# Moving the third h of a slot behind the next slot's W1 in a fused convolution and mixer kernel on Trainium2

## The chip, the cores and the metric

The kernel runs on one core of one Trainium2 chip. The metric is the device time of one execution in microseconds (us). Before the change the median of four runs is 327.03 us (326.15 to 327.87).

## What is computed

Two stages are fused. A causal convolution runs over the sequence with 7 taps per head (softmax of `weight`, 8 heads of 24 channels). Its output goes through a mixer with a low-rank part along the sequence and a two-layer part along the channels. Shapes: 8 batches, 4224 positions, 192 channels; rank 32, hidden width 768.

```python
w = softmax(weight, axis=-1)                      # 8 heads, 7 taps
y[b, s, h, :] = sum_k w[h, k] * x_pad[b, s + k, h, :]   # 6 zero rows ahead of x
xt = y.transpose(0, 2, 1)
h = xt @ U @ V                                    # rank 32, along the sequence
u = y + h.transpose(0, 2, 1)
out = u + np.maximum(u @ w_ch1, 0.0) @ w_ch2
```

## The kernel before, in words

**Tiles and groups.** The 8 x 4224 positions are cut into 264 tiles of 128 positions, 33 to a batch. Eight tiles make a group, so there are 33 groups (0 to 32), and some span two batches. For each batch there is a convolution (`c`), the product with U summed over the whole sequence (`t` and `s`), and for each group there are three steps:

- **h** (`h_group`, line 484, which calls `h_tiles`, line 442): eight matmuls (L453), two tiles to a PSUM bank, so four banks, or five where the first tile of the group is odd in its batch or the group spans two batches. Then VectorE adds y to each bank and writes u in bf16 (L475): one add for two tiles, or single adds where a run of four tiles ends. `transp` (L494) then issues one transposing DMA on SyncE's queue (SP), which gives uT.
- **W1** (`w1`, line 538): 36 matmuls of 512 columns (L550) from uT, in 12 banks, each cleared by a relu on ScalarE (L564) or VectorE (L566) after the pattern `RELU` (7 banks on ScalarE and 5 on VectorE).
- **W2** (`w2`, line 573): a group is done in four pieces. Each has 12 matmuls (L579) into one bank, one VectorE add of u that writes the output tile (L588), and one output DMA on SP (L596).

**Buffers.** All PSUM tiles come from one pool of 8 banks (`bank`, line 56), taken in turn in the order of the calls. A matmul into a bank waits until the tile that held it eight calls earlier has been read. u has 7 buffers, uT 5, y 3, relu outputs 3, output tiles 8.

**The order of the work is written out by hand** (`manual_schedule`). The list `SLOTS` (line 615) has 14 entries, counted here from 0. An entry names the groups whose W1 is run, then the groups whose W2 is run, and a dictionary of what stands ahead of which W2 piece. From slot 5 on a slot has W1 of three groups (3k-9 to 3k-7 for slot k), then the twelve W2 pieces of the same groups. The loop at line 786 runs W1 first, then for each position p what the dictionary gives for p, then piece p. In the codes `h9` is the h of group 9, `c4:0:3:AAD` the convolution of batch 4 for three heads from head 0 with its banks read by ScalarE, ScalarE, VectorE in turn (`conv32`, line 317: two banks and eight matmuls, L335, for each head; the reads are L252 and L254), `t4` and `s4` the low-rank sum, `x5:3` the first shifted copies of x on GpSimd. In slots 6 to 9 the convolution stands at positions 1, 2 and 3 (three, three and two heads), in slots 4 and 5 at 2, 3 and 4.

Before the change slot k, from 5 to 9, makes the h of groups 3k-5, 3k-4 and 3k-3 at positions 5, 8 and 11; position 11 is ahead of the last piece. Slot 4 makes h9 at position 11. Slots 10 to 12 have h at positions 0, 4 and 8.

**Loads.** x of a later batch is loaded by GpSimd's queue in four parts (`x_load`, L79), each held until a given block of W1 has ended (`LOADS`, line 666). Behind each load one more step of the shifted copies runs on GpSimd (L289, L301).

Of the kernel before, what the change touches and what calls it, by code (L numbers as in the profile page):

```python
# [14 lines left out]
def kernel(  # L15
# [590 lines left out]
    def x_load(b, q, after):  # L606
        if q == 0:
# [20 lines left out]
                6: ["t2"],  # L628
                8: ["s2"],
                9: ["h8"],  # L630
                11: ["h9"],
            },
        ),
    ]
    nh = 10
    for k in range(5, 14):
        gs = list(range(3 * k - 9, 3 * k - 6))
        hs = [f"h{g}" for g in range(nh, min(nh + 3, NG))] + [None] * 3
        nh = min(nh + 3, NG)
        if k == 5:  # L640
            at = {
                2: ["c3:0:3:AAD"],
                3: ["c3:3:3:AAD"],
                4: ["c3:6:2:A", "x4:3"],
                5: [hs[0]],
                6: ["t3"],
                8: ["s3", hs[1]],
                11: [hs[2]],
            }
        elif k < 10:  # L650
            b = k - 2
            at = {
                1: [f"c{b}:0:3:AAD"],
                2: [f"c{b}:3:3:AAD"],
                3: [f"c{b}:6:2:A"] + ([f"x{b + 1}:3"] if b + 1 < B else []),
                5: [f"t{b}", hs[0]],
                7: [f"s{b}"],
                8: [hs[1]],
                11: [hs[2]],
            }  # L660
        else:
            at = {0: [hs[0]], 4: [hs[1]], 8: [hs[2]]}
        SLOTS.append((gs, gs, {p: [w for w in what if w] for p, what in at.items()}))
# [176 lines left out]
```

## Time and profile before

| | |
|---|---|
| median of four runs | 327.03 us (326.15 to 327.87) |
| the profiled execution | 327.87 us, of which the profile's span is 326.1 us |
| granted TensorE clock, mean | 0.997 |
| TensorE weight loads | 223.6 us busy |
| ScalarE relu (L564) | 233 of 604 ns mean |
| VectorE relu (L566) | 163 of 688 ns mean |
| VectorE u add (L475) | 168 of 461 ns mean |
| VectorE output add (L588) | 133 of 551 ns mean |
| output DMAs | 131 issues, 2.9 us to landing |
| uT transposes | 31 issues, 4.1 us to landing |

The span runs from the first to the last instruction; the time of the run is a little longer than it. Busy time of an engine is what its instructions took. The chain that ended last follows the work back from the last instruction, at each step to what released it or to the instruction ahead of it on its engine. In the profile PE is the TensorE's matmuls, PEld its weight loads, DVE VectorE, ACT ScalarE, POOL GpSimd, SP SyncE; L550 is line 550.

### The profile page before, as it was taken

Reading aid. Unit: us, or ns where it says so; the run is one execution under the profiler, and the core shown is the slowest. Engines: PE = TensorE matmul, PEld = TensorE weight load, DVE = VectorE, ACT = ScalarE, POOL = GpSimd, SP = SyncE. Lnnn points to the kernel's source line nnn. Section 1 sums busy time; section 2 is a strip of 40 time slices with the busy share of each in tenths; the row PEclk is TensorE's granted clock in tenths of the full one; section 3 lists DMA queues with packets and bytes.
Section 4 is the critical chain, followed back from the end, with each engine's and each line's share of the span. In section 5 each row is a group of like instructions: output and inputs, shape, how many; then the busy total and the mean of one; then the engine's idle time right before and its main releaser. Section 6 shows DMA issues by size and latency. Waiting matters only on the chain.

```text
span 326.1 us, 9590 instructions
## 1 busy us (share of the span) xinstructions
PE 319.3 (98%) x3998; PEld 223.6 (69%) x3998; DVE 269.5 (83%) x552; ACT 170.0 (52%) x343; POOL 143.8 (44%) x112
## 2 busy tenths in 40 slices
PE   8999999999999999999999999999999999999994
PEld 3666676578677647866864784587796496497494
DVE  7659999986987987998798699879888888896853
ACT  1667524761775297088339609824904903903900
POOL 8584169717975894786859497000000000000000
PEclk9999999999999999999999999999999999999998
DMA  9999994999999999599799957139168079058044
GB/s 105 189 181 157 213 219 112 175 203 222 221 112 221 248 170 162 172 164 197 166 240 162 205 154 191 47 110 240 47 186 250 3 163 274 2 143 245 2 147 146
DMA packets 122907, 53.52 MB, mean 164 GB/s; under 512 B 87760, under 2 KB 122832, under 8 KB 122864
## 3 DMA queue, kind: packets, MB, share of 16 engines
q1 hardware_dynamic: 84528, 38.08, 48.0%
q0 software_dynamic: 38192, 14.73, 39.7%
q8 instruction: 31, 0.51, 0.6%
q14 instruction: 12, 0.10, 0.1%
q10 hardware_dynamic: 144, 0.10, 0.1%
HBM read 29.49 MB, written 25.95 MB: 170 GB/s over the span
## 4 chain that ended last, share of the span: by engine, by line
PE 91%; DVE 3%; DMA 3%; ACT 1%; issue 0%; POOL 0%; POOLq 0%
PE ps L579 41%; PE ps L550 39%; PE ps L335 3%; PE ps L453 3%; DMA x_sb<-in_x_dram 3%; PE ps L398 2%; DVE rl_sb L566 1%; ACT rl_sb L564 1%; DVE y_sb L254 1%; PE ps L365 1%; PE ps L505 1%; DVE u_sb L475 1%; PE ps L520 0%; ACT y_sb L252 0%; PE ps L678 0%
## 5 line engine op out<-in xcount | busy, mean ns | idle before, releaser
L564 ACT ACTIVATE rl_sb<-ps 128x512 bf16<-128x512 f32 x233 | 124.3, 604 | 108.0 <-PE ps L550 96.0
L579 PE MATMUL ps<-W_sb,rl_sb 128*128 128x192 bf16 x1584 | 141.9, 246 | 0.1
L579 PEld LDWEIGHTS <-rl_sb 128*128 128x128 bf16 x1584 | 128.0, 98 | 13.5 <-issue 13.0
L550 PE MATMUL ps<-uT,W_sb 64*128 64x512 bf16 x1188 | 131.8, 376 | 0.0
L566 DVE TENSOR_SCALAR rl_sb<-ps 128x512 bf16<-128x512 f32 x163 | 105.3, 688 | 15.7 <-PE ps L550 15.4
L550 PEld LDWEIGHTS <-W_sb 64*128 64x128 bf16 x1188 | 66.1, 94 | 61.4 <-issue 3.4
L588 DVE TENSOR_TENSOR out_sb<-ps,u_sb 128x384 f32<-128x384 f32 (+1 forms) x133 | 70.4, 551 | 25.8 <-PE ps L579 25.5
L301 POOL COPY xb_sb<-x_sb 32x3072 bf16<-32x3072 bf16 (+1 forms) x24 | 67.6, 2826 | 0.7
L475 DVE TENSOR_TENSOR u_sb<-y_sb,ps 128x192 bf16<-128x192 bf16 (+1 forms) x168 | 66.3, 461 | 0.0
L289 POOL COPY xb_sb<-x_sb 128x3072 bf16<-128x3072 bf16 x12 | 32.8, 2744 | 35.5 <-DMA x_sb<-in_x_dram 18.4
L252 ACT ACTIVATE y_sb<-ps 128x408 bf16<-128x408 f32 (+4 forms) x89 | 37.8, 512 | 11.1 <-PE ps L335 7.9
L79 POOL DMA_DIRECT2D x_sb<-in_x_dram x32 | 27.1, 851 | 16.9 <-PE ps L550 9.7
L254 DVE CAST y_sb<-ps 128x408 bf16<-128x408 f32 (+4 forms) x37 | 19.6, 578 | 1.4 <-PE ps L365 1.3
L453 PE MATMUL ps<-tt_sb,V_sb 32*128 32x192 bf16 x264 | 12.4, 246 | 0.2 <-DVE y_sb L254 0.2
L335 PE MATMUL ps<-xb_sb,band 64*32 64x384 bf16 x192 | 12.1, 332 | 0.0
L335 PE MATMUL ps<-x_sb,band 64*32 64x384 bf16 x192 | 12.1, 333 | 0.0
L453 PEld LDWEIGHTS <-V_sb 32*128 32x128 bf16 x264 | 4.7, 92 | 7.5 <-issue 7.5
L155 PE MATMUL ps<-zz 128*128 128x512 f32 x12 | 8.3, 846 | 1.5 <-DVE zz L145 1.5
L412 ACT ACTIVATE tt_hi<-ps 128x192 bf16<-128x192 f32 x8 | 2.6, 331 | 11.2 <-PE ps L398 11.1
L365 PE MATMUL ps<-x_sb,band 64*64 64x240 bf16 (+3 forms) x192 | 8.0, 275 | 0.4 <-DMA x_sb<-in_x_dram 0.4
L365 PEld LDWEIGHTS <-band 64*64 64x64 bf16 x192 | 6.0, 106 | 2.2 <-issue 1.8
L335 PEld LDWEIGHTS <-band 64*32 64x32 bf16 x384 | 4.5, 89 | 4.1 <-issue 3.0
(65 smaller groups left out, 73.8 us busy)
## 6 DMA issues: line engine op xcount, KB each, us to landing
out_dram<-out_sb SPq DMA_DIRECT2D x131, 192.0 KB, 2.9
x_sb<-in_x_dram POOLq DMA_DIRECT2D x14, 384.0 KB, 7.8
x_sb<-in_x_dram POOLq DMA_DIRECT2D x7, 432.0 KB, 7.8
x_sb<-in_x_dram POOLq DMA_DIRECT2D x7, 408.0 KB, 9.3
x_sb<-in_x_dram POOLq DMA_DIRECT2D x1, 504.0 KB, 8.8
uT<-u_sb SPq DMA_TRANSPOSE x31, 4.1
x_sb<-in_x_dram POOLq DMA_DIRECT2D x1, 480.0 KB, 5.8
W_sb<-in_moe_w_ch_dram POOLq DMA_DIRECT2D x2, 192.0 KB, 7.0
```

The costliest lines, as they stand in the source:

```text
L79: return nc.gpsimd.dma_start(out=xt[b][HB * r : HB * r + HB, s0:s1, :], in_=x[b, blk * HB : (blk + s1 - s0) * HB, :].rearrange("(j p) d -> ...
L252: nc.scalar.activation(out=out, in_=in_, func=ACT.Copy)
L289: nc.gpsimd.tensor_copy(out=xbt[b][:, s0:s1, :], in_=xt[b][:, s0 + 1 : s1 + 1, :])
L301: nc.gpsimd.tensor_copy(out=xbt[b][q, s0:s1, :], in_=xt[b][q, s0:s1, :])
L335: nc.tensor.matmul(out=pp[r][QB * cg : QB * cg + QB, 0 : nk[r] * GS], lhsT=w[hr], rhs=t[hr, st : st + 2 * nk[r] - 1 : 2, hs], start=True, ...
L453: nc.tensor.matmul(out=banks[pr][:, a * D : (a + 1) * D], lhsT=V_sb[32 * q : 32 * q + 32, (j // 8) * 2 + j % 2, :], rhs=ttb[b][32 * q : 32 ...
L475: nc.vector.tensor_tensor(out=u_group(g)[:, i : i + n, :, hf, :], in0=yt[b][:, run[0] : run[0] + n, :].rearrange("p n (c k) -> p n c k", c=3),
L550: last = nc.tensor.matmul(out=pps[m][hf][:], lhsT=W1_sb[HB * hf : HB * hf + HB, c, m * P : (m + 1) * P], rhs=uTt[g][HB * hf : HB * hf + HB ...
L564: nc.scalar.activation(out=rl[:, m, hf, :], in_=pp[hf][:], func=ACT.Relu)
L566: nc.vector.tensor_scalar_max(out=rl[:, m, hf, :], in0=pp[hf][:], scalar1=0.0)
L579: last = nc.tensor.matmul(out=cps[:, a * D : (a + 1) * D], lhsT=rlt[g][:, m, hf, (i + a) * P : (i + a + 1) * P], rhs=W2_sb[:, m, :], start ...
L588: nc.vector.tensor_tensor(out=o[:, 0:n, :].rearrange("p n (c k) -> p n c k", c=3), in0=cps[:, 0 : n * D].rearrange("p (n c k) -> p n c k", ...
```

## The change

Two things are changed in the table that orders the work. In slots 5 to 9 the h that stood at position 11 is no longer there, and one stands at position 0, between the last W1 and the first W2 piece of the slot. `nh`, the number of the first h that slot 5 makes, is 9 instead of 10, and slot 4 no longer has h9. So each h that stood at position 11 of a slot (groups 9, 12, 15, 18, 21, 24) stands at position 0 of the next one. The groups at positions 5 and 8 stay what they were. In slots 10 to 12 the numbers of the h are one lower at each position, and slot 12 has h32 at position 8 in place of 4. No instruction is added or taken away.

```diff
                 8: ["s2"],
                 9: ["h8"],
-                11: ["h9"],
             },
         ),
     ]
-    nh = 10
+    nh = 9
     for k in range(5, 14):
...
                 4: ["c3:6:2:A", "x4:3"],
-                5: [hs[0]],
+                0: [hs[0]],
+                5: [hs[1]],
                 6: ["t3"],
-                8: ["s3", hs[1]],
-                11: [hs[2]],
+                8: ["s3", hs[2]],
             }
         elif k < 10:
             b = k - 2
             at = {
+                0: [hs[0]],
                 1: [f"c{b}:0:3:AAD"],
                 2: [f"c{b}:3:3:AAD"],
                 3: [f"c{b}:6:2:A"] + ([f"x{b + 1}:3"] if b + 1 < B else []),
-                5: [f"t{b}", hs[0]],
+                5: [f"t{b}", hs[1]],
                 7: [f"s{b}"],
-                8: [hs[1]],
-                11: [hs[2]],
+                8: [hs[2]],
             }
```

## The prediction

> **What bounds the kernel now.** I read the busy table, then the chain that ended last, then single stretches of the timeline. Slots are numbered by their place in the list `SLOTS`, from 0; a "piece" is one call of `w2` (12 matmuls, 192 columns each).
>
> The page gives busy time by engine and the chain's shares:
>
> ```profile
> PE 319.3 (98%) x3998; PEld 223.6 (69%) x3998; DVE 269.5 (83%) x552; ACT 170.0 (52%) x343; POOL 143.8 (44%) x112
> ...
> PE 91%; DVE 3%; DMA 3%; ACT 1%; issue 0%; POOL 0%; POOLq 0%
> ```
>
> TensorE (PE) is the chain. From 69.20 us to 321.69 us the chain has no entry but PE, save 0.01 us of issue. So a moved step can gain only what PE loses next to it, and loses whatever PE is made to wait. The chain in order of time (start, length, what) gives the slots; L550 is W1, L579 a piece, L335 a convolution, L453 an h:
>
> ```profile
> 110.93 11.76 PE ps L550 x108
> 122.69 1.10 PE ps L579 x12
> 123.78 0.64 PE ps L335 x19
> 124.42 1.10 PE ps L579 x12
> ...
> 137.60 0.28 PE ps L453 x8
> 137.88 1.10 PE ps L579 x12
> 138.97 11.92 PE ps L550 x108
> ...
> 223.50 11.84 PE ps L550 x108
> 235.34 0.28 PE ps L453 x8
> 235.62 4.07 PE ps L579 x48
> ...
> 260.13 0.44 PE ps L453 x8
> 260.57 4.07 PE ps L579 x48
> ```
>
> The reader is to see three things. An h at the end of a slot costs PE its own 0.28 us (0.35 where its group spans two batches: 109.48 and 222.05). The W1 behind it takes 11.76 to 11.92 us. In slots 10 to 12 an h already stands right behind W1, and four pieces follow it without loss.
>
> **What the change moves.** No work is added or removed: 33 h, the same matmuls, adds and transposes. In slots 4 to 9 the h of position 11 (h9, h12, h15, h18, h21, h24) goes to position 0 of the next slot, past the last piece and three W1. Positions 5 and 8 keep the same groups. In slots 10 to 12 the h at positions 0, 4, 8 have numbers one lower, and h32 gets position 8 of slot 12.
>
> **What goes: the burst on VectorE (DVE) ahead of W1.** Its adds (about 2 us) run into W1's first microseconds there. Six W1 stand behind such an h, in slots 5 to 10: 11.92, 11.76, 11.92, 11.76, 11.76, 11.84 us. The W1 of slots 11 to 13, without one, take 11.76 each. The gain is 0.16 + 0.16 + 0.08 = **0.40 us** for the kernel, and it is also the most that these rows allow.
>
> **What comes: a burst on DVE right behind W1, and PSUM banks that are held by it.** The 8 banks go round in the order of the calls. After W1 the h takes 4 banks (h9, h18) or 5 (h12, h15, h21, h24, whose first tile is odd or which span two batches). The first piece takes one, and the convolution of three heads takes six. So the piece behind the convolution is the twelfth or thirteenth to ask, and gets the bank of the h's last add; two of the convolution's heads get h banks too. DVE first ends W1's relus, then does the adds, then the first piece's output. When do the adds end? Four slots already have h behind W1:
>
> - slot 10, four adds: h starts at 235.27, adds end 235.98 + 1.94 = 237.92, so 2.65 us after h's start
> - slot 12, six adds: 285.02 to 285.76 + 2.07 = 287.83, 2.81 us
> - slot 11, five adds: 2.75 us; slot 4, six adds: 65.90 to 66.61 + 2.07, 2.78 us
>
> In slots 10 to 12 four pieces follow h at once and ask only for free banks; that is why nothing is lost there. Slot 4 has a convolution after two pieces, and there the trace shows the mechanism. This is its timeline (start, length, engine, line, operation):
>
> ```profile
> 65.90 0.35 PE L453 MATMUL ps<-tt_sb,V_sb 32*128 32x192 bf16 x8
> 66.18 2.15 PE L579 MATMUL ps<-W_sb,rl_sb 128*128 128x192 bf16 x24
> 66.61 2.07 DVE L475 TENSOR_TENSOR u_sb<-y_sb,ps 128x192 bf16<-128x192 bf16 x6
> ...
> 68.60 1.02 DVE L588 TENSOR_TENSOR out_sb<-ps,u_sb 128x384 f32<-128x384 f32 x2
> ...
> 68.74 0.35 PE L335 MATMUL ps<-x_sb,band 64*32 64x384 bf16 x2
> ...
> 69.20 1.15 PE L579 MATMUL ps<-W_sb,rl_sb 128*128 128x192 bf16 x12
> ```
>
> The adds end at 68.68 and the convolution's third head goes on at 68.74 (0.06 us later). The first output add ends near 69.11, and the piece that gets its bank starts at 69.20 (0.09 us later). The convolution begins at 68.26 and takes 0.64 us where nothing stops it, so the piece could have started at 68.90: 0.30 us are lost although two pieces (2.09 us) lie between.
>
> Now the slots of the change, in us after h's start. In **slots 6 to 9** only one piece stands ahead of the convolution. PE gets through h, piece and convolution in 0.28 + 1.10 + 0.64 = 2.02. The next piece can't start before the last add, 2.81 + 0.06 = 2.87 with six adds (slots 7, 9), so 0.85 is lost in each. Slot 6 has six adds too, but h12 cost 0.35 where it was, so 0.78. Slot 8 has four adds: 2.65 + 0.06 - 2.02 = 0.69. In **slot 5** two pieces lie ahead, as in slot 4, and the third needs the first one's output add: 2.65 + 0.51 + 0.09 = 3.25, against 0.28 + 2.09 + 0.64 = 3.01, so 0.24. A wait of 0.16 us for h's fifth bank (slot 11 has 0.44 for such an h, not 0.28) ends before the add does, and is inside these numbers. In slots 10 to 12 the exchange of numbers comes to nothing: slot 10 gets the five-bank h (+0.16), slot 11 loses it (-0.16).
>
> Is something late after that? With six adds DVE does output 0 until 3.3, two casts of the convolution (0.52 each) until 4.3, output 1 until 4.8. The third piece asks for a cast's bank at 2.87 + 1.10 + 0.64 = 4.6, and gets it by 0.3 us. I take nothing here; if that cover goes, a second stall like slot 4's (0.30) comes in four slots, 1.2 us.
>
> Sum: 0.24 + 0.78 + 0.85 + 0.69 + 0.85 = 3.41 lost, 0.40 gained: **+3.0 us**.
>
> **What else moves.** Each moved h issues a transpose on SP (SyncE's queue). There it stood ahead of the slot's last output; now it stands ahead of the new slot's first. SP holds it until the adds end (2.8), issues for 1.3 to 2.6 us (the 31 transposes of the trace), then sends output 0 at 4.1 to 5.4. Outputs land in 2.9 us and have 8 buffers, so the first reuse comes eight pieces later, past 10 us: hidden by some 2 us. The transposed group is wanted by W1 of the next slot, a slot (28 us) later than the h. On POOL the loads of x are tied to W1's ends, and the last shifted copy ends at 123.05 against the convolution's start at 123.71 in slot 6. The convolution moves 0.28 us away from it, so that margin grows. POOL's wait ahead of its next load (1.18 us in slot 6) shrinks by the 0.35 us of the removed h at most. ScalarE is idle 0.81 us ahead of the convolution. All these cost nothing; if the tightest, SP's, failed, outputs would hold up DVE by what is over 2 us.
>
> **Two rules weighed.** The row is the slot 4 loss of 0.30 us with all banks in rotation. The Trainium skill, page "Perfetto Trace Analysis", section "Optimizing Tensor Performance", says that matmul groups which rotate through banks have their evacuation overlapped by the next group's matmuls. By that alone the change would cost nothing and give -0.4; the row decides against it, as rotation helps only while DVE is less than eight banks behind. The same page, section "Identifying the Most-Contended Engine", holds matmul busy time to be a poor measure and takes weight-load busy instead, which is 69% here and would leave room to absorb a wait. The row is W1's 11.76 us in slots 6, 8, 9 and 11 to 13, the same with and without DVE's burst: PE is at its pace, so I take a wait on PE in full.
>
> **Rivals.**
> - **A, the wait for h's adds** (forecast): +3.0.
> - **B, it is mostly covered**, each of five slots losing no more than slot 4's 0.30: 1.5 - 0.4 = +1.1. For it: that loss is the only one measured with a convolution behind h. Against: slots 6 to 9 have 1.1 us less cover.
> - **C, not slower: the adds end in time.** Place: the second piece of slots 6 to 9. It decides if the last add ends within 2.0 us of h's start; then only W1's gain is left, -0.4. Against: 2.65 to 2.81 in four slots. If, beyond that, h filled PE's gap at W1's end (weights for the first piece wait 0.42 us there), six times 0.28 more, -2.1. Against: in slots 10 and 11 W1 keeps its length and h is paid in full behind it.
> - **D, the stall carries on** into the third piece (the 0.3 us cover gone): +4.2.
>
> **How the numbers follow.** The sum stands against the profiled execution: span 326.1, time 327.87, so 330.9 after, span 329.1. That execution is the slowest of four; against the median, 327.03, the forecast is 327.03 + 3.0 = **330.0 us**. By the same base B gives 328.1, C 326.6 (or 324.9), D 331.2. Chances: A 0.68, D 0.14, B 0.09, C 0.05, its larger form 0.04. The 0.5% that a measurement of this kernel can tell from no change is 1.6 us. A and D are slower (0.82), B and C within (0.14), the larger C faster (0.04). The range takes A, B and D: 328.0 to 331.5, with 0.3 us for the runs' spread above D.
>
> **What would show it.** In the changed profile: W1 of slots 5 to 10 at 11.76 us. Behind each W1 an h of 0.28 to 0.44, a piece, and then in slots 6 to 9 a gap on PE of 0.7 to 0.85 us in or behind the first convolution, ended by DVE's L475, which will appear on the chain some 3 us more. In slot 5 a gap of 0.2 to 0.3 us, ended by L588. The forecast is wrong if the second piece starts within 2.1 us of h's start, if the gap comes again behind the second convolution, or if W1 falls below 11.76.

## The result, and the profile after

The changed kernel takes 327.77 us (median of 53 runs, 326.97 to 329.20), the kernel before 326.73 us (median of 79). The ratio is 1.0027, 95% interval 1.0020 to 1.0034: slower by 0.9 us, where 3.0 were forecast (the medians differ by 1.0). The profiled execution took 327.67 us, span 325.9. A few executions were in a second, slower state; the ratios leave them out, the medians of the later table do not (two of six executions in after_sp_plus, one of twelve in before_shifted and in late_mix).

The page after, the lines that answer to those of before (busy time by engine; the chain's shares):

```profile
PE 319.8 (98%) x3998; PEld 216.1 (66%) x3998; DVE 270.6 (83%) x552; ACT 170.1 (52%) x343; POOL 143.7 (44%) x112
...
PE 91%; DVE 6%; ACT 1%; issue 1%
```

PE is as busy as before; DVE has doubled its share of the chain, a first hint that PE now waits for it. The chain of the changed kernel in order of time (start, length, what) shows slot 6 and the first part of slot 10:

```profile
109.48 11.76 PE ps L550 x108
121.25 0.47 PE ps L453 x8
121.71 1.10 PE ps L579 x12
122.81 0.37 PE ps L335 x5
123.18 0.49 ACT y_sb L252
123.66 0.04 issue
123.71 0.36 PE ps L335 x5
124.07 1.10 PE ps L579 x12
...
134.10 4.07 PE ps L579 x48
138.16 11.76 PE ps L550 x108
...
224.11 11.76 PE ps L550 x108
235.87 0.53 PE ps L453 x8
236.40 4.07 PE ps L579 x48
```

The convolution behind the first piece, 0.64 us before, now takes 1.26 (122.81 to 124.07). What holds it is seen in the timeline of the same stretch (start, length, engine, line, operation):

```profile
121.65 1.16 PE L579 MATMUL ps<-W_sb,rl_sb 128*128 128x192 bf16 x12
121.92 2.07 DVE L475 TENSOR_TENSOR u_sb<-y_sb,ps 128x384 bf16<-128x384 bf16 x6
...
123.16 1.68 ACT L252 ACTIVATE y_sb<-ps 128x384 bf16<-128x384 f32 x4 [1.27 <-PE ps L335]
123.31 0.09 PEld L335 LDWEIGHTS <-band 64*32 64x32 bf16 x2 [0.42 <-DVE u_sb L475]
123.31 0.72 PE L335 MATMUL ps<-xb_sb,band 64*32 64x384 bf16 x2
...
123.71 0.35 PE L335 MATMUL ps<-x_sb,band 64*32 64x384 bf16 x2
...
123.91 0.55 DVE L588 TENSOR_TENSOR out_sb<-ps,u_sb 128x384 f32<-128x384 f32 x1
124.00 1.16 PE L579 MATMUL ps<-W_sb,rl_sb 128*128 128x192 bf16 x12
```

The third head of the convolution is torn in two. Its first matmul starts at 123.31, when one of VectorE's adds lets go of its bank (the weight load beside it had waited 0.42 us). The others start at 123.71, 0.05 us behind the end of ScalarE's first cast of this same convolution, which is the step that the chain names (to 123.66). Slots 7 and 9 show the same.

The adds end at 121.92 + 2.07 = 123.99 and the second piece starts at 124.00, but it doesn't wait for them: it starts 0.07 us ahead of the modelled end of the convolution (124.07), as it does in before, where nothing holds it (124.36 against 124.42). Slot 8, with four adds, shows this plainly:

```profile
179.36 1.94 DVE L475 TENSOR_TENSOR u_sb<-y_sb,ps 128x384 bf16<-128x384 bf16 x4
...
180.89 0.35 PE L335 MATMUL ps<-x_sb,band 64*32 64x384 bf16 x2
...
181.18 0.42 PE L579 MATMUL ps<-W_sb,rl_sb 128*128 128x192 bf16 x3
```

The last add ends at 181.30, and the piece has started at 181.18. The third head went on at 180.89, 0.05 us behind the end of the third add. Counted in turn, the piece would have had the bank of the last add. So the banks are not handed out strictly in turn, as the description of the kernel and the prediction have it; the trace doesn't tell which bank a call got. In slot 5 the wait is the one that was forecast: the third piece starts at 96.22, 0.05 us behind the end of the first piece's output add.

**Where the time went.** I compare TensorE from the first W1 of slot 4 to the start of slot 13's W1. From the two chains: before 297.93 - 57.80 = 240.13 us, after 298.93 - 56.96 = 241.97. So this stretch is 1.84 us longer, made up of:

| term | us |
|---|---|
| first convolution: 0.20 in slot 5, 0.62 in slots 6, 7, 9, 0.55 in slot 8 | +2.61 |
| h at position 0 takes 0.47 instead of 0.28 in slots 6, 7, 9 (waits for its fifth bank) | +0.57 |
| the other h, slots 4 to 12 | -0.05 |
| W1 of slots 5, 7, 10, now 11.76 | -0.40 |
| second convolution of slots 5 to 9: 0.71 to 0.64 | -0.34 |
| last four pieces of slots 5 to 9 in one run, 4.07 instead of 3.08 + 1.10 (in slot 4 the last three, 3.08 instead of 2.09 + 1.10); slot 12 gains such a break | -0.66 + 0.11 |

The rest of the time is the end. From the start of slot 13's W1 (its first matmul, 0.07 us ahead of the chain's entry) to the end of the span, before takes 28.22 us, after 27.01, with the same 12.00 us of pieces. +1.84 and -1.21 leave +0.6 in this pair of profiles. In the second pair below, +1.92 and -0.98 leave +0.9, which is the measured difference.

### The profile page after: what moved, and what is told of

It reads as the page before. It is cut to its first block, busy times and chain, and to the rows that moved or that the text cites. A ratio compares the mean times of both kernels' runs of the same rounds, so it can differ in the third digit from the quotient of the medians.

```text
span 325.9 us, 9590 instructions
## 1 busy us (share of the span) xinstructions
PE 319.8 (98%) x3998; PEld 216.1 (66%) x3998; DVE 270.6 (83%) x552; ACT 170.1 (52%) x343; POOL 143.7 (44%) x112
## 4 chain that ended last, share of the span: by engine, by line
PE 91%; DVE 6%; ACT 1%; issue 1%
PE ps L579 40%; PE ps L550 38%; PE ps L453 3%; PE ps L335 3%; PE ps L155 2%; DVE rl_sb L566 2%; PE ps L398 2%; DVE u_sb L475 2%; PE ps L365 1%; ACT rl_sb L564 1%; DVE y_sb L254 1%; PE ps L520 0%; ACT y_sb L252 0%; PE ps L505 0%; DVE out_sb L588 0%
## 5 line engine op out<-in xcount | busy, mean ns | idle before, releaser
L566 DVE TENSOR_SCALAR rl_sb<-ps 128x512 bf16<-128x512 f32 x163 | 106.8, 690 | 20.7 <-PE ps L550 20.5
L550 PEld LDWEIGHTS <-W_sb 64*128 64x128 bf16 x1188 | 58.3, 94 | 68.8 <-issue 2.7
L335 PE MATMUL ps<-xb_sb,band 64*32 64x384 bf16 x192 | 13.7, 332 | 0.4
```

The source lines that it names most:

```text
L335: nc.tensor.matmul(out=pp[r][QB * cg : QB * cg + QB, 0 : nk[r] * GS], lhsT=w[hr], rhs=t[hr, st : st + 2 * nk[r] - 1 : 2, hs], start=True, ...
L550: last = nc.tensor.matmul(out=pps[m][hf][:], lhsT=W1_sb[HB * hf : HB * hf + HB, c, m * P : (m + 1) * P], rhs=uTt[g][HB * hf : HB * hf + HB ...
L566: nc.vector.tensor_scalar_max(out=rl[:, m, hf, :], in0=pp[hf][:], scalar1=0.0)
```

## The experiments

"Chain" is the stretch above (slots 4 to 12); "end" runs from the start of slot 13's W1 to the end of the span. The ratio is against runs of the kernel before beside it.

| run | median us | ratio (95%) | chain | end |
|---|---|---|---|---|
| before, first profile | | | 240.13 | 28.22 |
| after, first profile | 327.77 | 1.0027 (1.0020-1.0034) | 241.97 | 27.01 |
| before_again | 326.92 | 0.9996 (0.9983-1.0010) | 240.05 | 27.99 |
| after_again | 327.36 | 1.0024 (1.0014-1.0034) | 241.97 | 27.01 |
| adds_to_copy | 325.80 | 0.9970 (0.9957-0.9983) | 239.71 | 27.00 |
| conv_one_later | 326.35 | 0.9989 (0.9975-1.0002) | 240.53 | 27.23 |
| before_shifted | 328.54 | 1.0033 (1.0009-1.0058) | 243.17 | 27.69 |
| h_behind_conv | 327.35 | 1.0012 (0.9993-1.0031) | 241.30 | 28.47 |
| h_ahead_of_w1 | 327.24 | 1.0006 (0.9989-1.0023) | 241.34 | 27.00 |
| conv_two_later | 327.24 | 1.0009 (0.9990-1.0028) | 241.37 | 27.00 |
| after_sp_plus | 328.54 | 1.0044 (1.0028-1.0060) | 241.94 | 27.45 |
| before_w_on_act | 326.94 | 1.0002 (0.9991-1.0014) | 240.83 | 28.17 |
| joined | 327.78 | 1.0029 (1.0015-1.0043) | 240.93 | 28.29 |
| late_mix | 326.79 | 0.9986 (0.9973-1.0000) | 239.60 | 28.01 |

**Both kernels once more** (before_again and after_again, no edit).

> The kernel before, once more, to see what differs between two executions of one program. Theory 1 (the order of the work sets the time of TensorE's chain, and start and end of an execution vary by chance): from the first W1 of slot 4 to the end of the last piece the chain takes the same 264.3 us within 0.2, while the start (first W1 of slot 4 at 57.7 us in the first profile) and the end (4.5 us behind the last piece) may differ by up to 1 us each. Rival (the profile of before is typical, and the change shortened start or end): start 57.7 and end 4.5 us again, within 0.2.

> The changed kernel, once more, for the same purpose. Theory 1: chain from W1 of slot 4 to the last piece 266.1 us within 0.2, the convolution behind the first piece of slots 6 to 9 at 1.2 us again; start and end within 1 us of the first profile's 56.9 and 3.2. Rival: start and end repeat within 0.2.

The chain repeats within 0.1 us in both. The start (the first W1 of slot 4), in a part of the program that the change leaves alone, went from 57.8 to 56.4 and from 57.0 to 56.3 us: chance. The end, though, repeated: 28.0 and 27.0. So the first half of theory 1 stands, and its word on the end falls: in both profiles of each kernel the changed one has the shorter end.

**The adds taken away** (adds_to_copy). In h_tiles, for groups 9, 12, 15, 18 and 21 (shortened; a copy takes up to four tiles at once):

```diff
-                nc.vector.tensor_tensor(out=u..., in0=yt..., in1=banks..., op=ALU.add)
+                nc.vector.tensor_copy(out=u..., in_=yt...)
```

> The changed kernel, in which the h of groups 9, 12, 15, 18 and 21 write u as a copy of y and leave out the added low-rank part: their matmuls stay, but no add reads their banks, and VectorE is done in about 0.7 us instead of 2.1. Theory 1 (the banks wait for VectorE's adds): the first convolution of slots 6 to 9 falls from 1.19 to 1.26 us to about 0.65, that of slot 5 from 0.84 to 0.65, and the time falls by about 2.9 us against the changed kernel, to some 324.9. Rival (the convolution is slow there because it follows the h on TensorE, whatever VectorE does): 1.2 us stays, and the time with it.

The chain of this kernel, slot 6 (L565 is W1 here, L455 the h, L594 the pieces):

```profile
109.27 11.76 PE ps L565 x108
121.03 0.47 PE ps L455 x8
121.50 1.10 PE ps L594 x12
122.59 0.64 PE ps L335 x19
123.23 1.10 PE ps L594 x12
124.33 0.71 PE ps L335 x17
```

The first convolution is 0.64 us right behind the same h and piece, so the order on TensorE costs nothing and DVE's adds cost it all. ScalarE's casts are the same here and the first convolution doesn't wait for them: its wait for a cast in slots 6, 7 and 9 comes only where the adds hold the other banks. Two more things are seen. The h keeps its 0.47: that wait is for W1's relus. And the second convolution is back at 0.71: its third head waits 0.07 us for ScalarE's casts whenever the first convolution isn't held. The chain fell by 2.26 us and not by the forecast 2.9, since that 0.07 came back five times.

**The convolution one piece later** (conv_one_later), in slots 6 to 9:

```diff
-                1: [c...], 2: [c...], 3: [c...], 5: [t, h], 7: [s], 8: [h]
+                2: [c...], 3: [c...], 4: [c...], 5: [h], 6: [t], 8: [s, h]
```

> The changed kernel with the convolution of slots 6 to 9 one piece later (positions 2, 3, 4, and behind it h, t, s as slot 5 has them). Theory 1: one more piece (1.09 us) hides the adds, so the first convolution of slots 6 to 9 takes 0.84 us as in slot 5, instead of 1.19 to 1.26; t and h no longer stand together, which costs one more switch of about 0.1 us in each slot; net 1.2 us less than the changed kernel, some 326.5. Rival (a fixed loss wherever a convolution follows within the slot): no change beyond 0.3 us.

The first convolution, to the start of the piece behind it, falls to 0.78 us in slots 6, 7 and 9 and 0.84 in slot 8, the chain by 1.44. One more piece of cover takes off 0.48 of 0.62 us, and 0.35 of 0.55 in slot 8: the cost is a matter of distance, not of a place in the slot. What is left is the wait of slot 5: the piece behind the convolution starts 0.05 us behind the end of the first output add.

**h ahead of W1** (h_ahead_of_w1): the kernel before with 11 changed to 12 in slots 4 to 9.

> The kernel before with the third h of slots 4 to 9 at position 12, between the last piece and the next W1, instead of 11. Theory 1 (TensorE pays about 0.1 us whenever it goes from pieces to matmuls on part of the rows, whatever VectorE does): the last pieces become one run of 4.07 us instead of 3.08 + 1.10, six times 0.11 less; W1 now meets the whole burst and grows by 0.5 to 1.0 us each, in slots 5 to 10; net 2 to 5 us slower than before, 329 to 332. Rival (the 0.11 us came from VectorE's burst beside the last piece): the four pieces take 4.18 in all.

In slots 5 to 9 the last four pieces are one run of 4.07 us, as theory 1 has it. This run alone doesn't refute its rival, as the adds now lie beside W1 and not beside a piece. Slots 10 to 12 of before do: there the adds lie beside the four pieces behind an h, and the four take 4.07. The weight loads of before show where the 0.11 goes:

```profile
134.45 2.92 PEld L579 LDWEIGHTS <-rl_sb 128*128 128x128 bf16 x36 [0.16 <-issue]
137.53 0.12 PEld L453 LDWEIGHTS <-V_sb 32*128 32x128 bf16 x8 [0.16 <-issue]
137.80 0.28 PEld L579 LDWEIGHTS <-rl_sb 128*128 128x128 bf16 x4 [0.16 <-issue]
```

They stand still for 0.16 us on the way from a piece (128 rows) to an h (32 rows), and again on the way back. The first is part of h's 0.28 us; the second makes the piece behind it 1.10 us instead of 0.99. So an h between pieces costs its 0.28 and 0.11 more. The sizes of theory 1 were off: W1 took 0.29 to 0.42 us more than 11.76, net 1.2 on the chain, and as the end is 27.0 us here, 0.3 in the median. The Trainium skill, page "TensorEngine Tiling (Array Packing)", section "Key Properties", says that changing the tiling mode drains the TensorE. These rows agree and give the price here, 0.10 to 0.11 us.

**h behind the convolution** (h_behind_conv): the changed kernel, slots 6 to 9, the third h from position 0 to 3.

```diff
-                0: [hs[0]],
-                3: [c...],
+                3: [c..., hs[0]],
```

> The changed kernel with the third h of slots 6 to 9 at position 3, right behind the convolution's last two heads, instead of position 0 (slot 5 and the rest as changed). Theory 1: no convolution follows the adds, so the first convolution is 0.65 us again (2.4 us less in four slots), the h costs 0.28 instead of 0.47 us in three of them, it shares the convolution's switch, W1 stays 11.76, and the second convolution goes back to 0.71: 2.7 us less than the changed kernel on TensorE's chain (239.3 us over slots 4 to 12 instead of 242.0), a time near 324.9, under that of before by 1.5 or more. Rival (VectorE has no room for the burst anywhere in these slots): the loss turns up at the sum t or at s, and the time stays above 326.5.

The expected 239.3 became 241.30. The h now waits, in the chain:

```profile
125.19 1.10 PE ps L579 x12
126.28 0.37 PE ps L335 x5
126.65 0.89 ACT y_sb L252 x2
127.54 0.04 issue
127.58 2.14 PE ps L579 x24
```

The h and the wait of the piece behind it take 0.90 us with five banks, the h 0.50 with four. The matmul into the fifth bank and then the piece each start 0.05 us behind the end of a cast of ScalarE, which has 12 of them in a row here (123.09 to 128.31). I had named the right thing, a bank whose reader is late, and looked at VectorE alone.

**The convolution two pieces later** (conv_two_later; in slots 5 to 9 conv at 3, 4, 5 with the second h behind its last heads, t with the third h at 7, s at 9, in slot 5 t at 7 and s with h at 9).

> The changed kernel with the convolution of slots 5 to 9 at positions 3, 4, 5, three pieces behind the h of position 0, the second h right behind its last heads, the sum t with the third h at 7 and s at 9 (slot 5: t at 7, s and h at 9). Theory 1: three pieces (3.2 us) hide the adds, so the first convolution takes 0.65 us in slots 5 to 9 (2.6 us less), one switch less in each slot (0.5 us less), the second convolution 0.71 again (0.35 more): 2.8 us less than the changed kernel, a chain of 239.2 us over slots 4 to 12, a time near 324.9. Rival (VectorE's load in the later half of the slot is then the bound): pieces or t behind position 7 grow, and the time stays above 326.

The first convolution is 0.64 us in all five slots, as forecast: three pieces hide the adds. But the h behind the convolution, with the wait of the piece behind it, takes 0.50 to 0.90 us for the reason just told, and the chain is 241.37 instead of 239.2.

**Joined and late_mix.** Both have the h of position 0, the convolution at 3, 4, 5 and t with the second h at 7, in slots 5 to 9. They differ in the third h:

```diff
-                9: [s, hs[2]],          # joined
+                9: [s], 10: [hs[2]],    # late_mix
```

> The changed kernel with the convolution of slots 5 to 9 at positions 3, 4, 5 with nothing behind it, the second h right behind t at 7 and the third right behind s at 9. Theory 1: the adds of the first h are over when the convolution starts (0.65 us instead of 0.84 to 1.26), no h stands right behind a convolution, where ScalarE's casts held its banks (0.9 instead of 0.28 us in the run with h behind the convolution), and the number of switches from pieces to narrower matmuls is that of the changed kernel: chain over slots 4 to 12 of 239.6 us against 242.0 changed and 240.1 before; time near 325.4 if the end takes 27.0 us as in the changed kernel, 326.4 if 28.0. Rival (VectorE or ScalarE can't follow so late in the slot): t, s or the pieces behind them grow, chain above 241.

> The run with joined steps, but the third h of slots 5 to 9 alone at position 10 instead of right behind s at 9. There an h two pieces behind the one before it took 0.68 to 0.80 us instead of 0.28 in three slots, because VectorE was still adding. Theory 1 (a step that takes four or five banks needs three pieces since the last such step): here one s and three pieces lie between, so the h takes 0.28, the first convolution 0.65 as three pieces lie between it and the h of position 0, W1 11.76; the chain over slots 4 to 12 is 239.5 us against 240.9 with joined steps and 240.1 before. The end takes 27.0 or 28.2 us, which this theory doesn't settle: time 325.2 or 326.3. Rival (the burst costs the same wherever it stands): chain 240.5 or more, a time of 326.7 or more.

With joined steps the rival is right in part. In slots 6, 8 and 9 the third h takes 0.80, 0.68 and 0.80 us from its start to that of the piece behind it (134.18 to 134.98 in slot 6). Slot 6's chain shows what it waits for:

```profile
132.39 0.80 DVE u_sb L475 x2
133.19 0.19 issue
133.38 1.07 DVE u_sb L475 x3
134.46 0.48 DVE out_sb L588
134.94 0.04 issue
134.98 3.13 PE ps L579 x36
```

Two pieces and s lie between two h, and the piece behind the second h starts only when the output add of an earlier piece, late behind the first h's adds, is done. With one more piece between (late_mix) these waits are gone, and so are those at the first convolution; the h at position 0 keeps its 0.47. The chain is 239.60 us, as forecast (239.5) and the shortest of the kernels that do all the work. Its median is 0.9986 of before (0.9973 to 1.0000), a gain at the edge of what can be told; against the changed kernel the chain is 2.4 us shorter.

**What sets the end.** Three runs were meant to move the last 8 KB fetch of instructions, with no change in the order of the work.

> The kernel before with extra instructions that nothing reads: eight loads of 28 bytes on SP at the start, and in slot 12 eight one-column memsets on VectorE and eight one-column copies on ScalarE beside the pieces. They move the place at which each engine's stream of instructions fetches its next 8 KB. In the two profiles of before such a fetch comes during the last outputs (322.4 of 326.1, 320.9 of 324.4 us) and a few packets of the last outputs trail the others by 1 us; in the two of the changed kernel it comes behind them, and the end is 1.0 to 1.2 us shorter. Theory 1 (the end depends on where the fetch falls, not on the order of the h): the fetch leaves the last outputs, from the start of W1 in slot 13 to the end takes 27.0 us instead of 28.0 to 28.2, and the time is 1 us lower than before, some 325.8. Rival (the end is shorter because of the order of the h and transposes): 28.0 stays, and the time is that of before within 0.3.

> The changed kernel with one more load on SP at the start, of 28 bytes that nothing reads, so that SP's stream is one or two instructions longer ahead of everything else. In the profiles the last 8 KB fetch of instructions goes out when SP passes a certain instruction of its closing waits: 24.5 us behind the start of slot 13's W1 in before (while the last outputs are under way), 25.5 us in the changed kernel (when they have landed). Theory 1 (the end depends on SP's place at that fetch): the fetch goes out at 24.4 to 24.5, the stretch from W1 of slot 13 to the end takes 28.0 us instead of 27.0, the time is 1.0 us more than the changed kernel's, some 328.5; the chain over slots 4 to 12 stays 242.0. Rival (the end is shorter because of where h32 and its transpose stand): 27.0 stays.

> The kernel before with the first small load (the convolution's weights, 28 KB) issued by ScalarE instead of SP, so that SP's stream is an instruction shorter. Theory 1: the last fetch goes out an instruction later, behind the wait for the last outputs (25.4 to 25.5 us behind slot 13's W1), the end takes 27.0 instead of 28.0 us, the chain stays 240.1, and the time is 1.0 us less than before, some 325.8. Rival: 28.0 stays, and the time is that of before.

None gave what theory 1 expected. before_shifted left the fetch among the last outputs (321.01 us, 21.1 behind the start of slot 13's W1) and lost 3.0 us on the chain besides, 1.8 of it in slots 4 and 5, where VectorE waited 2.27 us for an output buffer. after_sp_plus moved the fetch later, not earlier; its median of 328.5 us is the number that theory 1 gave, but the end is 27.45 and not 28.0, so that is luck. before_w_on_act left the fetch where it was, and the end with it (28.17), with 0.7 us more on the chain in slots 4 and 5. So an instruction more or less on SP didn't place the fetch as theory 1 has it. What the profiles do show is below.

## Why the prediction was wrong

The sign and the main mechanism held; the size failed, 0.9 us instead of 3.0. By its steps:

- **The wait at the banks**: right in cause and nearly in size. Forecast 0.24, 0.78, 0.85, 0.69, 0.85 us for slots 5 to 9; measured, with the h's own wait, 0.20, 0.81, 0.81, 0.55, 0.81. That is 3.18 against 3.41. adds_to_copy and conv_one_later show that the adds are the cause. The third piece of slots 6 to 9 didn't wait, as forecast.
- **"The next piece can't start before the last add"**: not so in slots 6 to 9. It was the convolution's third head that waited, at the end for a cast of ScalarE (slots 6, 7, 9) or for the third of four adds (slot 8), and the piece followed it without a wait. That the sizes agree in slots 6, 7 and 9 is in part luck: the rest of the third head happened to end when the last add did. In slot 8, where the last add ended later, 0.55 us were lost and not 0.69.
- **W1**: right, 0.40 us, and 11.76 in all six slots.
- **"An h at the end of a slot costs PE its own 0.28 us"**: wrong, and this is the step that failed on the chain. It also cost 0.11 us by breaking a run of pieces, while the first piece behind W1 takes 1.10 us with or without an h ahead of it. Six breaks less and one more: -0.55. The row was in front of me: 137.60 has h between runs, and slots 10 to 12 have 4.07 for four pieces.
- **A second convolution of 0.71**: not seen. I asked what is late after the stall, and not what is early: held up once, TensorE finds ScalarE's casts done, -0.34.
- **"The sum stands against the profiled execution: ... span 329.1"**: this took the end of the span as fixed. It got 1.0 to 1.2 us shorter, and that is half of the 2.1 us by which I missed. The prediction has no term for it, and what makes it shorter stays open (see the last section).
- **SP, POOL, ScalarE, and the slots 10 to 12**: no wait appeared on SP's or POOL's account. Slots 10 to 12 came to +0.39: 0.28 for one h more, 0.11 for the break, +0.25 and -0.16 for the five-bank h that slot 10 got and slot 11 lost, and -0.08 on slot 10's W1.

Rival B's 1.1 lies near the measured time, but its reason, five losses of 0.30, is not what happened.

## What to carry to other kernels

Price a moved step at both places, with what it breaks or joins there: the change of tiling mode, and the pace of the engines that catch up. Where many steps share a pool of buffers, ask which step needs one while a late reader still holds it, look at every engine that reads them, and read in the trace what really ended each wait; three pieces (3.1 us) between two steps of 2 us of adds were enough here, two were not. Compare the start and the end of the span separately from the stretch that was changed, and over more than one profile.

## What the runs showed of the hardware beyond that

In most profiles the end of the span has one of two lengths, and they go with the place of one 8 KB transfer on the queue that the page calls "instruction". The DMA view of before, 322 to 326 us (busy share and GB/s in 40 slices of 0.1 us), and of after, 323 to 327:

```profile
DMA  0069999999999300000000000000000000000000
GB/s 0 0 223 420 346 353 361 331 338 338 346 353 307 85 8 8 8 23 23 23 15 31 15 23 23 15 0 0 0 0 0 0 0 0 0 0 0 0 0 0
...
out_dram<-out_sb SPq DMA_DIRECT2D x1, 96.0 KB, 3.0
```

```profile
DMA  0069999999999500000000000000000003000000
GB/s 0 8 230 361 369 369 369 377 361 369 369 369 307 159 0 0 0 0 0 0 0 0 0 0 0 0 0 0 0 0 0 0 0 82 0 0 0 0 0 0
...
out_dram<-out_sb SPq DMA_DIRECT2D x1, 96.0 KB, 1.7
```

In before the last outputs trickle on at 8 to 31 GB/s, after some 350, for 1.2 us, and the one shown lands after 3.0 us; in after they end at once, and it lands after 1.7. The slow rate is about what one of 16 DMA engines would give (350 / 16 = 22, an estimate), but the profile names no engine. The trace puts the instruction transfer 24.5 us behind the start of slot 13's W1 in before, before_again, before_w_on_act and late_mix, and 25.1 in joined: the end is 28.0 to 28.3 in all five. In after, after_again, h_ahead_of_w1 and conv_two_later it comes at 25.5 to 25.6, when the outputs have landed: 27.0 in all four. adds_to_copy and conv_one_later have no such transfer before 27.4 us, and ends of 27.00 and 27.23. Three profiles are apart: before_shifted (21.1, end 27.69), and h_behind_conv (25.5, end 28.47) and after_sp_plus (25.8, end 27.45), in which the outputs land as early as in after but SP's closing steps come late. h_ahead_of_w1 has the order of before from slot 11 on and the short end, joined has that of after and the long one, so the place of h32 doesn't decide it. That the fetch holds up one DMA engine would fit the first nine but wasn't shown by moving it; what places it stays open.
